# A chunked state-space scan and a two-layer MLP in one kernel: chunks 1 and 2 made one unit of work

## The chip, the core and the metric

The kernel runs on one core of a Trainium2 chip. The metric is device time in microseconds of one execution, the median over several runs. The engines are named as in the profile: PE is TensorE (PEld its weight loads), DVE is VectorE, ACT is ScalarE, POOL is GpSimd, SP is SyncE, which here only issues DMA transfers. A q after a name means the engine's instruction queue.

## What is computed

The first stage is a linear recurrence over a sequence, done in chunks; the second is a two-layer MLP with a tanh GELU on its output.

```python
batch, n_heads, seq, head_dim, d_state = (4, 8, 768, 32, 16)
n_tokens, d_model, d_ff = (3072, 256, 2048)

log_a = np.log(np.clip(a, 1e-06, 1.0))
for c in range(nc):                       # chunks of the sequence
    cum = np.cumsum(la, axis=-1)
    L = np.exp(cum[:, :, :, None] - cum[:, :, None, :]) * causal
    CB = np.einsum('bhin,bhjn->bhij', Cc, Bc)
    y_intra = np.einsum('bhij,bhjd->bhid', CB * L, xc)
    y_inter = np.einsum('bhin,bhnd->bhid', Cc, state) * np.exp(cum)[:, :, :, None]
    y[:, :, sl] = y_intra + y_inter
    Bx = np.einsum('bhjn,bhjd->bhjnd', Bc, xc) * decay_from_j[:, :, :, None, None]
    state = decay_full[:, :, None, None] * state + np.sum(Bx, axis=2)

h = x @ w_in                              # x: y with tokens as rows, 256 wide
g = 0.5 * h * (1.0 + np.tanh(c * (h + 0.044715 * h * h * h)))
out = g @ w_out
```

## The kernel before

The kernel uses its own chunk length, Q = 128, so each of the 4 batches has 6 chunks and there are 24 in all. Chunks are grouped in units: chunks 0 to 3 one by one, then pairs. `UNITS` (L120) holds the grouping, `UOF` the unit of a chunk.

The decays are not formed as exponentials of differences. For each row of a (32 batch-head rows) a reversed scan of products within a chunk gives r; C is divided by r and B multiplied by it, so that a plain product of the two with a triangular mask is already the decayed matrix. For batch 0 this is done for each half of the sequence (three chunks) separately: the four blocks of decay rows are loaded by `load_a3` (L160, DMA at L157), clipped (`f_clip3`, L304), scanned (`f_R3`, L300), transposed (`f_RT3`, L313), inverted (`f_recip3`, L317) and multiplied into C and B (`f_mul3`, L360). For batches 1 to 3 the same is done at once from `load_a12` (`f_clip12`, `f_R12`, `f_RT12`, `f_recip12`, `f_mul`).

PE then transposes C and B (`f_T3`, L371; for whole batches `f_T`, L407). The results are copied out as bh (`f_E0`, `f_E`) and, once for even and once for odd heads, as ce (`f_F0` at L389 on ACT or L391 on DVE; `f_F`). A transposed copy of bh, bn, comes from `f_N` (L426) and `f_bn`.

For each unit there follow: `f_castx` (x to 16 bits), `f_G` (the Gram product of B and C, L461, into the PSUM tile gb), `f_M` (gb times the triangular mask, L471, on DVE), `f_D` (the chunk's addition to the state, L482), `f_S` and `f_SP` (the state and its product with the block mask, L531 and L538, on DVE), `f_Y` (L504 for the part from the state, L513 for the part within the chunk, into the PSUM tile yb) and `f_yev` (its evacuation to xm, the MLP's input). `f_pe`, `f_pp` and `f_pend` form the decay of a whole chunk for the state.

gb has four banks; in each, half of the columns serve one chunk. In this version chunk 0's product goes into the left half and chunk 1's into the right half, both made in one step (`f_G(0)` calls `f_G(1)`, and `half` chooses the side).

The MLP's first layer is `f_s1` (L562): for a unit of one chunk, matmuls of 128 columns, for a pair 256; four or eight PSUM tiles per unit, each emptied by one GELU on ACT (`f_gelu`, L571). The second is `f_s2` (L580), four pieces for each chunk, then `f_oev` (evacuation) and `f_store`. The weights are loaded in 32 bits and cast to 16 by `f_wi` and `f_wo`, in eight pieces each, by POOL, ACT or DVE.

The order on each engine is not written by hand. Each step is a `Node` with an assumed duration, dependences and a priority; `run_order` simulates the engines with these durations and emits the steps in the order it finds. Dependent steps in the planner are not waits on the chip; what is emitted is each engine's order, and the chip waits by data. `TUNE` gives each step's priority by name (lower goes first among those ready), for loads (`ad_...`) too, where it overrides the order of `FIRST`; `ENG` gives the engine of a step that has a choice, and without an entry it is the first of its options: POOL for casts of weights and of x, ACT for F0 and bn and the evacuation of Y, DVE for E0 and E. All loads are issued on SP, save six of the eight row blocks of a for batch halves 0 and 1, which are issued on ACT. The loads before are in this order: C and B of the first half, w_in rows 128 to 255, x of chunk 0, w_in rows 0 to 127, x of chunk 1, C of the second half, x of chunk 2, B of the second half, the decays of all batches, two quarters of w_out, x of chunk 3, two quarters of w_out.

Where PE has nothing to do in the plan before the first `f_s1`, `idle` puts in filler matmuls (L836), one per 0.07 us of planned idle time (0.107 before 4.4 us). `paced` is a table of steps: after such a step's planned end the fillers read a tile that the step writes, and so can't start earlier on the chip. Before, the three steps are the clip, scan and transpose of the first half's decays. Fillers write a part of yb or, for a time, of gb.

Of the kernel before, what the change touches and what calls it, by code (L numbers as in the profile page):

```python
# [9 lines left out]
BF16 = mybir.dt.bfloat16  # L10
# [83 lines left out]
def kernel(  # L94
# [10 lines left out]
    nc = tc.nc  # L105
# [5 lines left out]
    NCH = batch * CPB  # L111
    HS = S // 2
    R3 = HS // 128
    R12 = S // 64
# [5 lines left out]
    UNITS = [[c] for c in range(4)] + [[c, c + 1] for c in range(4, NCH, 2)]  # L120
# [24 lines left out]
    XF, X16 = {}, {}  # L145
# [25 lines left out]

    wz = const.tile([128, 512], BF16, name="wz")
# [4 lines left out]
    for q in range(4):  # L177
        load_a3(1, q, nc.scalar)
# [274 lines left out]
    def half(u):  # L453
        return 1 if u == 1 else 0

    def f_G(u):
        if u == 0:
            f_G(1)
        for k, gc in enumerate(UNITS[u], half(u)):
            for g in range(4):  # L460
                nc.tensor.matmul(  # L461
                    out=gb[:, g, 256 * k:256 * k + 256],
                    lhsT=bh_of(gc)[32 * g:32 * g + 32],
                    rhs=ce_of(gc)[32 * g:32 * g + 32],
                    start=True, stop=True, tile_position=(32 * g, 0))

    def f_M(u, k, g0, g1):
        gc = UNITS[u][k]
        if g0 == 0:
            MT[gc] = msb.tile([128, 4, 2, Q], BF16, name="m")  # L470
        nc.vector.tensor_tensor(out=MT[gc][:, g0:g1],  # L471
                                in0=gb[:, g0:g1, 256 * (k + half(u)):256 * (k + half(u)) + 256]
                                .rearrange("p g (e t) -> p g e t", e=2),
                                in1=tri_b[:, g0:g1], op=ALU.mult)
# [145 lines left out]

    def load(dur, fn, *args, deps=()):
        nload[0] += 1
        return add("DMA", dur, fn, *args, deps=deps, done=0.9, prio=nload[0])

    win_l, won_l, wi_n, wo_n = {}, {}, {}, {}
    bl, bl3, xl, xcn = {}, {}, {}, {}
    Gn, Mn, Dn, Yn, yevn, Sn, SPn = ({} for _ in range(7))
    cen, bhn, bnn = {}, {}, {}

    a3n = load(2.6, landed, "a0")  # L630
    a3n.done = 0.8
    a3n1 = add("SP", 6.2, landed, "a1", done=0.9, prio=-1)

    FIRST = "C30 B30 i0 x0 i1 x1 C31 B31 x2 o0 x3 o1 o2 o3 A x4 x5"
    for item in FIRST.split() + [f"{t}{b}" if t in "CB" else f"x{CPB * b + int(t)}"
                                 for b in range(1, batch) for t in "CB012345"]:
        t, i = item[0], int(item[1:] or 0)
        if t in "CB" and i >= 30:
            bl3[i - 30, int(t == "C")] = load(1.0, load_bc3, i - 30, int(t == "C"))
        elif t in "CB":  # L640
            bl[i, int(t == "C")] = load(1.2, load_bc, i, int(t == "C"))
        elif t == "A":
            a12n = load(1.7, load_a12)
        elif t == "x":
            xl[i] = load(1.0, load_x, i)
        elif t == "i":
            win_l[i] = load(2.65, load_wi, i)
        else:
            won_l[i] = load(1.35, load_wo, i)
# [11 lines left out]
    for k in range(2):  # L661
        z = 60.0 * k
# [35 lines left out]
    def half_sequence(k):  # L698
        z = 40.0 * k
        t1 = add("PE", 0.2, f_T3, k, 1, deps=[mul3[k, 1], Gn.get(2)], prio=-70 + z)  # L700
        t0 = add("PE", 0.2, f_T3, k, 0, deps=[mul3[k, 0], t1], prio=-69 + z)
        if k == 0:
            T0n.append(t0)
        ev = {"ACT": 0.6, "DVE": 0.52}
        f = [add(ev, 0, f_F0, k, 0, deps=[t1], prio=-70 + z)]
        f.append(add(ev, 0, f_F0, k, 1, deps=[t1, f[0]], prio=-70 + z))
        e0 = add({"DVE": 0.52, "ACT": 0.6}, 0, f_E0, k, deps=[t0], prio=-70 + z)
        nn = add("PE", 0.2, f_N, 0, k, deps=[e0], prio=-25 + z / 4)
        bb = add({"ACT": 0.5, "DVE": 0.36}, 0, f_bn, 0, k, deps=[nn], prio=-20)
        if k:  # L710
            t1.takes("gram", *f, e0, bb)
        else:
            t1.takes("o", *f)
            t0.takes("yb", e0)
            nn.takes("hp", bb)
        for c in range(k * CPB // 2, (k + 1) * CPB // 2):
            cen[c], bhn[c], bnn[c] = f, e0, bb


    for u, cs in enumerate(UNITS):  # L720
# [8 lines left out]
        if u <= MERGE:  # L729
            gn = Gn[u] = Gn[0] if u == 1 else add(  # L730
                "PE", 0.2 + 0.11 * (2 if u == 0 else n), f_G, u, deps=cen[cs[-1]] + [bhn[cs[-1]], Gn.get(u - 1)], prio=-60 if u < 2 else q)
            Dn[u] = add("PE", 0.2 + 0.03 * n, f_D, u, deps=[bnn[cs[0]], xcn[u]], prio=q + 0.5)
            if u == 0:
                Dn[u].deps.append(Gn[u])
        else:
            gn = Gn[u] = Dn[u] = Yn[u - 1]
            gn.deps += cen[cs[-1]] + [bhn[cs[-1]], bnn[cs[0]], xcn[u]]
# [8 lines left out]
        if u == 1:  # L746
            gn.allocs[0][1].extend(ms)
        else:
            gn.takes("gram", *ms)
        Mn[u] = ms  # L750
        ss = []
        for k, gc in enumerate(cs):
            if gc % CPB == CPB - 1:
# [119 lines left out]
```

## Time and profile before

| | us |
|---|---|
| median of 13 runs | 125.15 |
| lowest and highest | 124.06, 127.96 |
| the profiled execution, its own time | 124.36 |
| span of its instructions | 122.2 |

| engine | busy us | share of the span |
|---|---|---|
| PE | 113.4 | 93% |
| PEld | 100.8 | 82% |
| ACT | 78.6 | 64% |
| DVE | 68.6 | 56% |
| POOL | 16.7 | 14% |

The profile is of one execution. The span leaves 2.16 us of that execution outside. A share of busy time is an average over the fill-in of the pipeline, the long stretch in which PE runs the MLP beside the rest, and the end. A slice of the page's second part is a fortieth of the span, 3.06 us, and its digit the busy share in tenths. PE's busy time holds the fillers too.

### The profile page before, as it was taken

What the parts mean: (1) busy time and instruction counts of PE and PEld (TensorE: products, weight loads), DVE (VectorE), ACT (ScalarE), POOL (GpSimd) and SP (SyncE); (2) the same over time, 40 slices, a digit from 0 to 9 for tenths busy, and PEclk for the clock granted to TensorE, in tenths of its full rate; (3) what the DMA queues carried; (4) which work ended last, traced back from release to release, by engine and by line L of the source; (5) the groups of instructions that cost most, each with busy time, mean ns of one, the idle gap of its engine ahead of it and who ended that gap; (6) DMA issues with size and microseconds to landing.
All of it is one profiled execution on the core that took longest, in us unless ns stands there. A gap on an engine that the chain in (4) does not pass through costs nothing.

```text
span 122.2 us, 3590 instructions
## 1 busy us (share of the span) xinstructions
PE 113.4 (93%) x1531; PEld 100.8 (82%) x1531; DVE 68.6 (56%) x127; ACT 78.6 (64%) x152; POOL 16.7 (14%) x34
## 2 busy tenths in 40 slices
PE   4992899889999999999999999999999999999990
PEld 4981787769878897998889997989898899999970
DVE  5927957999968895570899452756657200000100
ACT  4153547987674786778765675767576877678510
POOL 7204312521442042021200000000000000000000
PEclk9999769999999999999999999999999999999999
DMA  1999479999989898995011101110111011110021
GB/s 41 270 353 334 73 171 343 374 236 140 168 206 207 146 157 230 136 176 129 5 38 48 43 0 48 43 43 5 46 43 48 6 42 43 43 43 30 18 86 43
DMA packets 37199, 14.23 MB, mean 116 GB/s; under 512 B 29952, under 2 KB 36416, under 8 KB 36928
## 3 DMA queue, kind: packets, MB, share of 16 engines
q1 hardware_dynamic: 36896, 13.87, 46.3%
q8 instruction: 12, 0.20, 0.7%
q10 hardware_dynamic: 288, 0.14, 0.5%
q14 instruction: 3, 0.02, 0.1%
HBM read 10.85 MB, written 3.15 MB: 115 GB/s over the span
## 4 chain that ended last, share of the span: by engine, by line
PE 81%; DVE 7%; DMA 5%; issue 2%; ACTq 2%; ACT 1%; DVEq 0%
PE hp L562 32%; PE o_ps L580 31%; DMA a_t<-in_a_dram 5%; PE yb L580 3%; PE gb L461 3%; PE yb L513 2%; PE yb L504 2%; PE yb L836 2%; PE gb L407 2%; ACTq L157 2%; DVE r_t L300 1%; PE o_ps L562 1%; DVE sp_new L538 1%; DVE m L471 1%; PE gb L426 1%
## 5 line engine op out<-in xcount | busy, mean ns | idle before, releaser
L571 ACT ACTIVATE gT<-hp 128x512 bf16<-128x512 f32 x94 | 52.2, 596 | 18.0 <-PE hp L562 17.9
L562 PE MATMUL hp<-xm,w_in_sb 128*128 128x256 bf16 (+1 forms) x432 | 51.3, 261 | 0.0
L580 PE MATMUL o_ps<-w_out_sb,gT 128*128 128x256 bf16 x352 | 46.9, 273 | 0.5 <-DVE w_out_sb L289 0.5
L562 PEld LDWEIGHTS <-w_in_sb 128*128 128x128 bf16 x448 | 43.0, 115 | 2.9 <-issue 1.9
L580 PEld LDWEIGHTS <-gT 128*128 128x128 bf16 x384 | 37.1, 98 | 4.5 <-issue 0.7
L471 DVE TENSOR_TENSOR m<-gb,tri 128x1024 bf16<-128x1024 f32 (+1 forms) x25 | 29.3, 1172 | 1.8 <-PE gb L461 1.7
L589 DVE COPY o_sb<-o_ps 128x256 f32<-128x256 f32 x3 | 1.3, 425 | 23.4 <-PE o_ps L580 23.4
L287 POOL CAST x<-x_t 128x512 bf16<-128x512 f32 (+1 forms) x11 | 8.2, 741 | 26.0 <-DMA x_t<-in_x_dram 17.1
L285 ACT ACTIVATE xm<-yb 128x512 bf16<-128x512 f32 (+1 forms) x13 | 7.1, 548 | 5.6 <-PE hp L482 4.0
L836 PEld LDWEIGHTS <-wz 128*128 128x128 bf16 x95 | 8.5, 131 | 2.3 <-DVE warm L175 1.5
L538 DVE SCALAR_TENSOR_TENSOR sp_new<-s_new,pend,bmask 128x256 bf16<-128x256 f32 x20 | 10.2, 512 | 0.1
L531 DVE SCALAR_TENSOR_TENSOR s_new<-s_new,pend,hp 128x64 f32<-128x64 f32 x16 | 4.5, 280 | 10.0 <-PE hp L482 9.7
L836 PE MATMUL yb<-wz 128*128 128x128 bf16 x73 | 7.8, 282 | 2.0 <-DVE warm L175 1.6
L587 ACT ACTIVATE o_sb<-o_ps 128x256 f32<-128x256 f32 x19 | 7.3, 384 | 3.0 <-ACT gT L571 2.2
L513 PE MATMUL yb<-m,x 128*32 128x128 bf16 x192 | 6.3, 220 | 0.0
L504 PE MATMUL yb<-ce,sp_new 128*32 128x128 bf16 x160 | 5.4, 222 | 0.0
L399 DVE TENSOR_TENSOR bc<-bc_t,rt 128x1536 bf16<-128x1536 f32 x3 | 5.3, 1752 | 0.2 <-DMA bc_t<-in_B_dram 0.2
L461 PE MATMUL gb<-ce,bh 32*128 32x256 bf16 x96 | 5.1, 278 | 0.1
L513 PEld LDWEIGHTS <-x 128*32 128x32 bf16 x192 | 3.8, 96 | 0.7 <-issue 0.6
L504 PEld LDWEIGHTS <-sp_new 128*32 128x32 bf16 x160 | 2.8, 96 | 1.9 <-issue 1.7
L287 POOL CAST w_out_sb<-wf 128x512 bf16<-128x512 f32 x5 | 3.1, 638 | 7.6 <-DMA wf<-in_moe_w_out_dram 7.6
L289 DVE COPY ch<-gb 128x768 bf16<-128x768 bf16 x2 | 1.9, 957 | 3.7 <-PE gb L407 3.7
(78 smaller groups left out, 69.1 us busy)
## 6 DMA issues: line engine op xcount, KB each, us to landing
x_t<-in_x_dram SPq DMA_DIRECT2D x24, 128.0 KB, 4.7
out_dram<-o_sb SPq DMA_DIRECT2D x24, 128.0 KB, 1.7
wf<-in_moe_w_in_dram SPq DMA_DIRECT2D x2, 1024.0 KB, 7.7
wf<-in_moe_w_out_dram SPq DMA_DIRECT2D x4, 512.0 KB, 5.1
bc_t<-in_C_dram SPq DMA_DIRECT2D x3, 384.0 KB, 4.6
bc_t<-in_B_dram SPq DMA_DIRECT2D x3, 384.0 KB, 6.1
bc<-in_C_dram SPq DMA_DIRECT2D x2, 192.0 KB, 5.5
bc<-in_B_dram SPq DMA_DIRECT2D x2, 192.0 KB, 3.8
```

Source lines behind the costliest of these rows:

```text
L285: nc.scalar.activation(o, i, AF.Copy)
L287: nc.gpsimd.tensor_copy(out=o, in_=i)
L461: nc.tensor.matmul(out=gb[:, g, 256 * k:256 * k + 256], lhsT=bh_of(gc)[32 * g:32 * g + 32], rhs=ce_of(gc)[32 * g:32 * g + 32], start=True, ...
L471: nc.vector.tensor_tensor(out=MT[gc][:, g0:g1], in0=gb[:, g0:g1, 256 * (k + half(u)):256 * (k + half(u)) + 256] .rearrange("p g (e t) -> p ...
L504: nc.tensor.matmul(out=y4[32 * j:32 * j + 32, k, w], lhsT=sp[:, 32 * h:32 * h + 32], rhs=ce_of(gc)[:, h % 2], start=first(j), stop=False, ...
L513: nc.tensor.matmul(out=y4[32 * j:32 * j + 32, k, w], lhsT=X16[u][:, k, 32 * h:32 * h + 32], rhs=m[:, h // 2, h % 2, :], start=first(j), st ...
L538: nc.vector.scalar_tensor_tensor(out=sp_new.rearrange("p (g d) -> p g d", g=4), in0=state[("s", gc)].rearrange("p (o d) -> p o d", o=1).to ...
L562: nc.tensor.matmul(out=hp[:, j * nt:(j + 1) * nt], lhsT=w_in_sb[:, kc].rearrange("p (q m k) -> p q k m", m=128, k=4) [:, fi // 4, fi % 4], ...
L571: nc.scalar.activation(gts[u][:, i * per:(i + 1) * per, 0:nt], hps.pop((u, i)).rearrange("p (j t) -> p j t", j=per), AF.Gelu_apprx_tanh)
L580: nc.tensor.matmul(out=ops[gc], lhsT=gts[u][:, fi, tt * Q:(tt + 1) * Q], rhs=w_out_sb[:, fi, :], start=(fi == 0), stop=(fi == NF - 1), ski ...
L587: nc.scalar.activation(o_sb, ops.pop(gc), AF.Copy)
L836: nc.tensor.matmul(out=(gb[:, 3] if g_next else yb)[:, 384:384 + w], lhsT=wz[:, 0:128], rhs=r, start=True, stop=True)
```

## The change

The two chunks 1 and 2 become one unit, as the later pairs are. Chunk 0's and 1's Gram products are still made in one step; chunk 2's is made in a step of its own, into the left half after chunk 0's mask product has read it. The four row blocks of the second half's decays are issued on ACT's queue directly after those of the first half, ahead of the warm activation and its table load. Fillers are also paced by the cast of chunk 0's x, the two halves of its mask product and the eight casts of w_in. The planner is given other durations for three loads, and new tables of priorities and engines.

```diff
-    UNITS = [[c] for c in range(4)] + [[c, c + 1] for c in range(4, NCH, 2)]
+    UNITS = [[0], [1, 2], [3]] + [[c, c + 1] for c in range(4, NCH, 2)]
...
+    for q in range(4):
+        load_a3(1, q, nc.scalar)
+
     wz = const.tile([128, 512], BF16, name="wz")
...
     nc.scalar.activation(warm, warm, AF.Gelu_apprx_tanh)
-    for q in range(4):
-        load_a3(1, q, nc.scalar)
...
-    def half(u):
-        return 1 if u == 1 else 0
+    def slot(gc):
+
+        return 1 if gc == 1 else 0 if gc == 2 else UNITS[UOF[gc]].index(gc)

     def f_G(u):
-        if u == 0:
-            f_G(1)
-        for k, gc in enumerate(UNITS[u], half(u)):
+        for gc in {0: [0, 1], 1: [2]}.get(u, UNITS[u]):
+            k = slot(gc)
...
-                                in0=gb[:, g0:g1, 256 * (k + half(u)):256 * (k + half(u)) + 256]
+                                in0=gb[:, g0:g1, 256 * slot(gc):256 * slot(gc) + 256]
...
-    a3n1 = add("SP", 6.2, landed, "a1", done=0.9, prio=-1)
+    a3n1 = add("SP", 7.2, landed, "a1", done=0.9, prio=-1)
...
-            bl3[i - 30, int(t == "C")] = load(1.0, load_bc3, i - 30, int(t == "C"))
+            bl3[i - 30, int(t == "C")] = load(1.2, load_bc3, i - 30, int(t == "C"))
...
-        t1 = add("PE", 0.2, f_T3, k, 1, deps=[mul3[k, 1], Gn.get(2)], prio=-70 + z)
+        t1 = add("PE", 0.2, f_T3, k, 1, deps=[mul3[k, 1], Gn.get(1)], prio=-70 + z)
...
-    paced = {cl3n[0]: ac3[:, 0, 0:128], R3n[0]: r3_t[:, 0, 0:128],
-             RT3n[0]: rt3[:, 0].rearrange("p r b -> p (r b)")}
+    paced = {cl3n[0]: lambda: ac3[:, 0, 0:128].bitcast(BF16)[:, 1::2],
+             R3n[0]: lambda: r3_t[:, 0, 0:128].bitcast(BF16)[:, 1::2],
+             RT3n[0]: lambda: rt3[:, 0].rearrange("p r b -> p (r b)").bitcast(BF16)[:, 1::2],
+             xcn[0]: lambda: X16[0][:, 0, 0:128]}
+    for i in range(2):
+        paced[M0n[i]] = lambda i=i: MT[0][:, 2 * i, 0]
+    for q in range(4):
+        for k in range(2):
+            paced[wi_n[q][k]] = lambda q=q, k=k: w_in_sb[:, k, 512 * q:512 * q + 128]
```

By the new priorities the loads stand in this order: C and B of the first half, x of chunk 1, w_in rows 128 to 255, x of chunk 0, x of chunk 2, w_in rows 0 to 127, B and C of the second half, the decays of all batches, one quarter of w_out, x of chunk 3, three quarters of w_out.

The entries of the engine table, before and after (`wi_q_k` and `wo_q_k` are the casts of the weights in pieces; the rest of them is on POOL):

```
before  ACT: wi_0_1 wi_1_0 wi_3_1 wo_0_1 wo_3_1 castx_0 castx_1 castx_3 E_1_1 E_1_0
        DVE: wi_2_0 wo_2_0 yev_1 F0_1_1 oev_2
after   ACT: wi_1_0 wi_2_1 wi_3_0 wi_3_1 wo_3_1 E_1_1 E_1_0
        DVE: F0_0_0 F0_0_1 F0_1_0 F0_1_1 bn_0_1 bn_1_None
```

## The prediction

> **What bounds it.** I read the page's slices first, then the chain of waits, then the timeline of the first 36 us.
>
> ```profile
> PE   4992899889999999999999999999999999999990
> DVE  5927957999968895570899452756657200000100
> PEclk9999769999999999999999999999999999999999
> DMA  1999479999989898995011101110111011110021
> ```
>
> A slice is 3.06 us. From the tenth slice on TensorE (PE) never lets go; 93% of the span is PE. What can be won lies before 28 us: the fill-in of the pipeline, with a clock that drops in slices 5 and 6 (7 and 6 tenths) and a full VectorE (DVE) in slices 8 to 11. The chain, in order of time, shows how it starts:
>
> ```profile
> 3.43 6.30 DMA a_t<-in_a_dram
> 9.82 0.27 DVE ac L304
> 10.11 0.87 DVE r_t L300
> ...
> 13.93 1.64 PE yb L836 x14
> 15.57 0.33 PE gb L461 x3
> 15.90 0.98 PE o_ps L562 x8
> 16.87 1.20 PE hp L562 x16
> ```
>
> The last row block of the second half's decays is issued at 3.43 and lands at 9.73. DVE sits 1.76 us idle for it although the first Gram product ended at 8.78, so the first mask product M (L471) starts only at 11.74. Then 14 fillers (L836) run 117 ns each, and the first dense layer ("s1", L562) starts at 15.83. The windows give the clock:
>
> ```profile
> 7.10:10.50 3.40, 2.23 (x36) 1.59 (x34) 1.21 (x3) 2.04 (x5) 0.54 (x1) 1.00 1.04 373
> 10.50:13.90 3.40, 1.78 (x29) 1.48 (x30) 3.33 (x9) 1.47 (x6) 1.80 (x4) 1.00 0.84 188
> 13.90:17.30 3.40, 3.38 (x32) 2.96 (x32) 2.58 (x5) 1.19 (x3) 0.65 (x2) 0.51 0.61 121
> ```
>
> The eighth number is the clock: half speed for one stretch of 3.4 us, after one in which PE was busy 1.78 us only. Later:
>
> ```profile
> 26.95 0.43 DVE L289 CAST w_out_sb<-wf 128x512 bf16<-128x512 f32 x1
> 27.43 0.60 PE L580 MATMUL o_ps<-w_out_sb,gT 128*128 128x256 bf16 x4 [0.47 <-DVE w_out_sb L289]
> ```
>
> This w_out quarter landed at 23.9; its cast stood in DVE's queue for 3 us, and the second layer ("s2", L580) with it. Likewise the first quarter landed at 20.4, was half cast by ScalarE (ACT) at 23.42, and s2 began at 24.02.
>
> **The Trainium skill.** "TensorE: Matmul & The Clock Gate", section "What's actually happening": the clock is halved after a free-running window of about 3.4 us with too little matmul work and restored after a busy one. The windows above agree: 0.51 for 3.4 us. "DMA: Bandwidth & Descriptors", section "Queues, rings and completion order": each DMA engine takes turns between the issuing queues by packet and drains one queue in order. So rows issued on ACT do not stand wholly behind the SP loads, but share with them; the four blocks took 2.6, 3.2, 5.3 and 6.3 us, growing once w_in (1 MB, issued at 2.80) is in flight. "SBUF — State Buffer", section "Who interferes with whom": DVE operations with two SBUF inputs and GpSimd (POOL) reads exclude each other. The trace agrees: the scan takes 0.56 us alone and 0.86 beside POOL casts, the state product 0.48 and 0.82.
>
> **Part by part.**
> Decay rows: four ACT issues move ahead of the table load and the warm activation. Issues are 0.44 apart, so the sixth starts near 3.0 instead of 3.43. Landing: at best 3.0 + 5.3 = 8.3, at worst 9.7 as before; I take 8.9. The table load (1.28) slips to about 3.5 to 4.8 and the warm 0.20 to 5.0; cover is ACT's idle until 5.74.
>
> First Gram product: both copies of C (F0) go from ACT (1.05 for two) to DVE at 0.62 each (row L391), then B's copy 0.55: 7.03 + 1.79 = 8.8 against 8.06. The Gram ends 0.7 later, 9.2; hidden, since DVE clips (0.26) and scans (0.56 to 0.86) then anyway. M's two halves now stand behind the scan but before the transpose, reciprocal and pe pair: 8.9 + 0.26 + 0.86 + 1.28 + 0.15 = 11.45 done, against 13.15.
>
> Loads: x of chunk 1 goes ahead of the first w_in half, x of chunk 2 ahead of the second. Each x costs 0.43 to 0.49 where one followed w_in (10.33 after 9.9, 13.37 after 12.88). So w_in lands at 10.4 and about 13.8 instead of 9.9 and 12.88, worth +0.9 (bounds 0.5 to 1.3). B before C of the second half: both were waited for by nothing until 17.09, and their last landed at 16.8. The same loads stand before w_out; bounds for it 0.5 later to 1.5 earlier (the SP queue sat blocked while DMA moved 13 to 170 GB/s between 12.5 and 15.5). I take no change. x of chunk 3 ahead of the second w_out quarter: +0.45 there, covered as that quarter's cast ended at 23.0 and s2's second piece ran at 25.03.
>
> Casts: x of chunks 0 and 1 move from ACT to POOL, behind two w_in casts (0.61 each, 0.88 at most): 10.4 + 1.3 + 0.40 = 12.1, so Y of chunk 0 at 12.2 (was 13.08) and its evacuation at 13.0 (13.87). The last w_in casts: two on POOL, two on ACT from 13.8, first pair done 14.45; the one on DVE until 14.74 goes.
>
> Fillers: none after chunk 0's evacuation is tied to a step until w_in's last casts; I estimate some 25 of them, from about 13.1, at 56 ns (the 0.90 of 16 matmuls at 28.91), with the state-decay product pp waiting in between for DVE until about 14.4. s1 starts at 15.2; bounds 14.5 (cast alone) and 16.2 (fillers at 117 ns). Gain **0.63**. Tied to M's halves, the x cast and the w_in casts, the fillers spread over 10 to 12.3, where before there was nothing from 9.33 to 11.66. By my count of 18 fillers (1.0), products (0.5) and fillers after 13.1 (0.8), the bad window holds 2.3 us of issue instead of about 1.4. Then the clock stays up: the first 24 s1 matmuls took 0.98 + 1.20 = 91 ns each, at 56 they save 24 x 35 = **0.84**.
>
> The unit of two: Y needs both mask products, both states. DVE from 11.45: two M 2.44, transpose 0.30, reciprocal 0.29, pe pair 0.57, states 0.21 + 2 x 0.28, state products 3 x 0.48, hops 0.5 = 6.3, so Y at 17.8 and evacuation done at 19.1 (one ACT copy of 0.60 for two of 0.38 and 0.42). Chunk 1's s1 began at 19.24 before, so it loses nothing, and chunk 2's evacuation ended at 20.87: 1.7 earlier. PE waits about 1.3 us between s1 of chunk 0 (done 17.0) and 19.1. The Gram of chunk 2 goes into the half whose M is done; no cost shown or taken (0 to 0.3, waiting for a reader of the same bank). 64 narrow matmuls at 56 ns (3.58 us) become 32 of 256 columns at 109 (0.87 for 8 in the chain; 3.49): **0.09**.
>
> 19 to 28: issue work on PE from 18.07 to 28.03 was 72 x 0.056 + 12 x 0.109 + 2.1 of attention = 7.5, so 2.5 us were idle. In place of it: the 1.3 above, and 0.7 for ACT's pace (eight gelus of 0.57 for eight s1 of 0.44, s2 pieces between). w_out is cast by POOL but for one: quarters ready at 21.6, 23.1, 25.2 and 27.2, so s2 can begin 2.4 earlier and the wait on DVE at 27.43 goes. Gain 2.5 - 2.0 = **0.5**, bounds -0.4 to 1.5. ACT loses F0, x and bn work there; DVE gets the other F0 and two bn copies (0.62 + 0.49 + 0.9), loses three casts and an evacuation (0.42 each or so).
>
> Sum: 0.63 + 0.84 + 0.5 + 0.09 = 2.06. Profiled execution 124.36 (span 122.2 and 2.16 around it): 122.3. The median 125.15 lies 0.79 higher, part of it perhaps the clock window's phase that this removes; I add half: **122.7**.
>
> **Rivals.** First, a wash: PE arrives earlier and waits for chunks 4 and 5. Their x landed at 29.96 and took POOL 1.98; Y (0.45) and evacuation (0.60) make 33.0, PE would want s1 at 35.5 - 2.0 = 33.5. With x 1 us later half a us goes, with DVE's extra copies the rest; or the fillers run cold again (s1 at 16.2, no clock gain) and only the 19 to 28 gain is left. 124.2 to 125.5. For it: slack of only 0.5. Against: 1.75 us of s2 for chunk 3 lay in reserve there.
>
> Second, slower: chunk 1 is tied to chunk 2's M, last in DVE's line. If the second half's two decay products (0.55 each), the clip, the scan or its copies go ahead of it, Y slips from 17.8. It decides from about 20.3, where the old chunk 2 stood. PE has no s1 from 17.0 on; an empty stretch of over 2.3 us (the one before the drop at 13.9) costs the clock, as it did then: 3.4 us at half speed, 1.7 of work. Y at 21.5 gives 124.4 + 1.2 + 1.7 - 0.8 = 126.5. For it: DVE is full from 21.4. Against: B and C of the second half land near 16.
>
> Third, the rows don't land earlier (9.7): M done 12.3, but the x cast at 12.1 bounds Y anyway; 122.9.
>
> **Numbers.** Main case and its third variant 0.60, wash 0.13, slower 0.27. A measurement here tells about 0.5% from no change, 124.5 to 125.8. Faster 0.60, same 0.13, slower 0.27. The main case alone spans 120.6 (s1 at 14.5, idle 1.0) to 124.0; with the rivals 120.6 to 126.4.
>
> **What would show it.** Right: clip of the second half before 9.2, no clock below 0.9 after 10 us, s1 from about 15.2, no DVE casts of weights, s2 from about 21.7. Wrong: a half-speed stretch between 13 and 21, Y of the pair after 20, or PE idle near 33.

## The result, and the profile after

The change makes the kernel slower: 127.17 us median of 11 runs (125.55 to 127.92, and one at 149.82), beside 125.21 for the kernel before in 48 runs. The ratio of their runs is 1.0151, 95% interval 1.0112 to 1.0191. I had forecast 122.7 and given a slower kernel 0.27. A ratio leaves out the runs that lie well above the fastest of their own kernel, so it can part from the medians, the more so where a kernel has few runs; where the two differ below, both are given, and where they disagree on the sign no gain is taken.

The profiled execution took 127.15 us with a span of 125.3, against 124.36 and 122.2: the span is 3.1 us longer. (The execution profiled before was 0.8 faster than its median, so this pair shows some 1 us more than the medians do.) First the same four rows of the page, of the kernel after (a slice is now 3.13 us):

```profile
PE   5985888959699995999999999999999999999980
DVE  5796968981979269935499480928475300000110
PEclk9999999999999999999999999999999999999999
DMA  2998979999799799995011101100111011111021
```

In this execution the clock never falls, as I said. But TensorE is not closed from the tenth slice on as it was: slices 9, 11 and 16 are a 5, a 6 and a 5. VectorE's tenth and fourteenth slices are a 1 and a 2 (9 and 8 before), and the DMA engines are busy into the eighteenth slice, as before. What TensorE waits for between 24 and 52 us, in the kernel after (total, times, longest):

```profile
PE o_ps L581 <- POOL w_out_sb L288: 1.4, 2, 1.2
PE gb L408 <- DVE bc L400: 1.0, 1, 1.0
PE yb L514 <- DVE m L472: 0.8, 1, 0.8
PE yb L505 <- DVE sp_new L539: 0.4, 1, 0.4
```

Together 3.6 us. The same question to the trace of before gives one row, for the cast of w_out that the prediction showed:

```profile
PE o_ps L580 <- DVE w_out_sb L289: 0.5, 1, 0.5
```

So the waits of this stretch have grown by 3.1 us, as much as the span. Up to 24 us the kernel after is not behind: its second layer begins at 22.33, before at 24.02. The chain of the kernel after says what stands behind each (start, us, what):

```profile
6.17 4.52 SPq L276
...
12.49 2.59 SPq L157
...
19.81 11.04 DMA bc_t<-in_C_dram
30.97 1.77 DVE bc L400
32.78 0.84 PE gb L408 x12
...
39.12 5.91 DMA bc_t<-in_B_dram
45.06 1.76 DVE bc L400
46.82 1.13 DVE m L472
```

Where the chain of before ran over VectorE and TensorE from 10 us on, this one is a queue of loads until 31 us and again from 39 to 45. SyncE (SP) sits 4.52 us in the issue of the second half of w_in. The multiply of a batch needs its C and its B. The later of the two for batch 1 is now C, at 30.85 (before it was B, at 29.18), and for batch 2 B, at 45.03 (40.64 before). VectorE stands idle for each, with the rest of its queue behind; before, the first of these multiplies started at 29.75 without a wait. After, then before:

```profile
30.97 1.76 DVE L400 TENSOR_TENSOR bc<-bc_t,rt 128x1536 bf16<-128x1536 f32 x1 [3.27 <-DMA bc_t<-in_C_dram]
...
45.06 1.76 DVE L400 TENSOR_TENSOR bc<-bc_t,rt 128x1536 bf16<-128x1536 f32 x1 [2.24 <-DMA bc_t<-in_B_dram]
```

```profile
29.75 1.75 DVE L399 TENSOR_TENSOR bc<-bc_t,rt 128x1536 bf16<-128x1536 f32 x1
```

Why B of batch 2 is so late: the new priorities put five loads of x between C of batch 2 and it, where before there was one (its issue is at 39.12, before at 34.83). Two expectations below say seven; the trace shows five. Landing times of the early loads, read from the trace:

| landed at, us | before | forecast | after |
|---|---|---|---|
| last row block of the second half's decays | 9.73 | 8.9 | 6.25 |
| w_in, first and second half issued | 9.90, 12.93 | 10.4, 13.8 | 10.82, 15.29 |
| w_out, four quarters | 20.36, 21.62, 23.94, 25.92 | no change | 19.82, 23.85, 25.08, 27.41 |
| C and B of batch 1 | 27.56, 29.18 | not treated | 30.85, 29.39 |
| C and B of batch 2 | 38.15, 40.64 | not treated | 36.57, 45.03 |

### The profile page after: what moved, and what is told of

Its sections match the earlier page's. It is cut to its first block, busy times and chain, and to the rows that moved or that the text cites. A ratio compares the mean times of both kernels' runs of the same rounds, so it can differ in the third digit from the quotient of the medians.

```text
span 125.3 us, 3575 instructions
## 1 busy us (share of the span) xinstructions
PE 113.5 (91%) x1527; PEld 99.8 (80%) x1527; DVE 69.1 (55%) x128; ACT 75.9 (61%) x145; POOL 19.4 (16%) x38
## 4 chain that ended last, share of the span: by engine, by line
PE 62%; DMA 15%; SPq 13%; DVE 6%; issue 1%; ACT 0%; ACTq 0%; DVEq 0%
PE hp L563 25%; PE o_ps L581 25%; DMA bc_t<-in_C_dram 9%; DMA bc_t<-in_B_dram 5%; SPq L276 5%; SPq L157 3%; DVE bc L400 3%; PE yb L581 3%; PE gb L462 2%; PE yb L514 2%; DVE m L472 2%; PE yb L505 2%; PE gb L408 2%; SPq L268 2%; DMA a_t<-in_a_dram 2%; SPq L282 1%
## 5 line engine op out<-in xcount | busy, mean ns | idle before, releaser
L572 ACT ACTIVATE gT<-hp 128x512 bf16<-128x512 f32 x94 | 52.3, 596 | 17.8 <-PE hp L563 17.6
L563 PEld LDWEIGHTS <-w_in_sb 128*128 128x128 bf16 x416 | 41.4, 114 | 3.9 <-issue 1.9
L288 POOL CAST x<-x_t 128x512 bf16<-128x512 f32 (+1 forms) x13 | 9.8, 762 | 26.5 <-DMA x_t<-in_x_dram 16.6
L590 DVE COPY o_sb<-o_ps 128x256 f32<-128x256 f32 x2 | 0.8, 424 | 23.0 <-PE o_ps L581 23.0
L844 PEld LDWEIGHTS <-wz 128*128 128x128 bf16 x123 | 9.2, 115 | 3.2 <-DVE warm L178 1.5
L844 PE MATMUL yb<-wz 128*128 128x128 bf16 x74 | 6.4, 250 | 1.6 <-DVE warm L178 1.6
L288 POOL CAST w_out_sb<-wf 128x512 bf16<-128x512 f32 x7 | 4.3, 631 | 5.5 <-DMA wf<-in_moe_w_out_dram 5.5
L530 DVE COPY s_new<-hp 128x64 f32<-128x64 f32 x4 | 0.9, 225 | 7.1 <-PE hp L483 7.1
```

The costliest lines, as they stand in the source:

```text
L288: nc.gpsimd.tensor_copy(out=o, in_=i)
L563: nc.tensor.matmul(out=hp[:, j * nt:(j + 1) * nt], lhsT=w_in_sb[:, kc].rearrange("p (q m k) -> p q k m", m=128, k=4) [:, fi // 4, fi % 4], ...
L572: nc.scalar.activation(gts[u][:, i * per:(i + 1) * per, 0:nt], hps.pop((u, i)).rearrange("p (j t) -> p j t", j=per), AF.Gelu_apprx_tanh)
L844: nc.tensor.matmul(out=(gb[:, 3] if g_next else yb)[:, 384:384 + w], lhsT=wz[:, 0:128], rhs=r, start=True, stop=True)
```

## Experiments

My theory after this: the order of loads that came with the change costs the time, and the three parts that the change is named for (unit of two, early rows, pacing) do not. The main rival: the unit of two, with the copies and casts that were spread anew for it, costs it. All times below are medians beside the median of the kernel before in the same series. The series ran on five chips, and the kernel before gave 124.74 to 125.07 in them, so a difference of a few tenths between two series says nothing.

| run | edit | runs | us | before | ratio, 95% interval |
|---|---|---|---|---|---|
| e1 | after, x of chunk 2 behind w_in | 4 | 127.48 | 125.07 | 1.0161, 0.9996 to 1.0327 |
| e2 | after, B of batch 2 early | 4 | 125.50 | 125.07 | 1.0109, 1.0013 to 1.0204 |
| e3 | before, rows early | 6 | 125.50 | 125.07 | 1.0127, 1.0018 to 1.0236 |
| e4 | before, more paced steps | 20 | 124.81 | 125.07 | 1.0000, 0.9960 to 1.0040 |
| e5 | before, x of chunks 1, 2 early | 22 | 125.49 | 124.80 | 1.0042, 1.0008 to 1.0077 |
| e6 | after, all priorities of loads of before | 6 | 128.86 | 124.80 | 1.0323, 1.0254 to 1.0392 |
| e7 | after, old three paced steps | 6 | 126.39 | 124.80 | 1.0124, 1.0051 to 1.0197 |
| e8 | e3 and e4 together | 22 | 125.14 | 124.80 | 0.9928, 0.9888 to 0.9968 |
| e9 | before, B of batch 2 late | 6 | 129.81 | 125.04 | 1.0400, 1.0333 to 1.0467 |
| e10 | e5 and e9 together | 6 | 131.11 | 125.04 | 1.0482, 1.0408 to 1.0556 |
| e11 | e8, w_out ahead of later decays | 22 | 124.75 | 125.04 | 0.9928, 0.9889 to 0.9967 |
| e12 | after, both loads put back | 22 | 125.37 | 125.04 | 1.0072, 1.0038 to 1.0106 |
| e13 | before, without 1 MB of w_out | 6 | 124.49 | 125.06 | - |
| e14 | e8, without it | 6 | 121.86 | 125.06 | 0.9743, 0.9702 to 0.9784 |
| e15 | after, without it | 6 | 123.68 | 125.06 | 0.9875, 0.9835 to 0.9915 |
| e16 | e12, without it | 6 | 122.83 | 125.06 | 0.9827, 0.9784 to 0.9870 |
| e17 | e8, two w_out quarters on ACT's queue | 22 | 125.00 | 124.74 | 0.9969, 0.9913 to 1.0025 |
| e18 | e12, the same | 14 | 125.16 | 124.74 | 1.0057, 1.0019 to 1.0095 |

Where only loads move, the plan of all engines stays and SP's issues alone are permuted:

```diff
-    for t, fn in run_order(nodes, pools, idle=idle, wait=("DVE", "POOL")):
-        fn()
+    plan = run_order(nodes, pools, idle=idle, wait=("DVE", "POOL"))
+    loads = sorted((n for n in nodes if n.name.startswith("ad_")), key=lambda n: n.start)
+    want = [n.name for n in loads]
+    for m, after in MOVES:
+        want.remove(m)
+        want.insert(want.index(after) + 1, m)
...
+    plan = [swap.get(fn, fn) for _, fn in plan]
```

### One load at a time (e1, e2)

```diff
+    MOVES = [('ad_x_2', 'ad_wi_0')]             # e1, in the kernel after
+    MOVES = [('ad_bc_2_0', 'ad_bc_2_1')]        # e2, in the kernel after
```

> The changed kernel with one load moved on SP's queue: x of chunk 2 issued behind the second half of w_in instead of ahead of it; the order on every other engine stays. Theory (the load order holds the issue of w_in's second half back until the first half has landed, and everything behind it on DMA comes later): that w_in half is issued near 5.5 instead of 6.2 to 10.7, lands near 13.4 instead of 15.3, the first dense layer starts near 15.3 instead of 16.2, w_out's last quarter and C of batch 1 land 1 to 1.5 us earlier, and the time falls by 1.5 to 2.5 us. Rival (the unit of two and the copies given to DVE cost the time, not the loads): the first layer may start earlier, but the waits near 28 and 32 us stay and the time stays within 0.6 us.

> The changed kernel with one load moved on SP's queue: B of batch 2 issued directly behind C of batch 2, ahead of the x of chunk 12 and six more chunks. Theory (the two waits of PE at 48 to 50 us, 0.60 and 1.00, come from that load landing at 45.0): B of batch 2 lands before 41, both waits go, 1.6 us less. Rival (other work on DVE is the bound there): the load lands earlier and the waits remain, no change.

e2's trace did what was expected: B of batch 2 landed at 38.77, and the waits at 47 to 50, 1.2 us in the rows above, are gone. How much that is worth is less sure. The median of its four runs is 1.67 below that of the kernel after, but by the ratios (1.0109 and 1.0151, with intervals that overlap) the gain is only some 0.5. In the profiled execution the wait for the cast of w_out grew by as much as the others had been; the last quarter landed at 28.19 there, after at 27.41 (TensorE's waits, 24 to 52 us):

```profile
PE o_ps L581 <- POOL w_out_sb L288: 2.6, 2, 2.2
```

In e1 the half of w_in landed at 13.05, as expected, but the first dense layer did not follow: it began at 18.53. GpSimd takes its casts in order, and the cast of x of chunks 1 and 2 stands ahead of the last w_in casts in the plan. It now waited for the later x (landed 14.44), the w_in casts behind it ended at 16.29, and TensorE stood before the state product of that x:

```profile
PE hp L483 <- POOL x L288: 2.8, 1, 2.8
```

With the clock gone too, e1's start is 2.4 us later than that of the kernel after; yet its profiled execution took 125.55, less than the 127.15 of after. It is the fastest of e1's four, whose median (127.48) is no better than that of the kernel after, so no gain is shown. But within this one execution the start comes later and the end sooner: a first sign that the start does not set the end.

### The other two parts alone (e3, e4, e7, e8)

```diff
     for q in range(4):
         load_a3(0, q, nc.scalar if q in (1, 2) else nc.sync)
+    for q in range(4):                          # e3 and e8, in the kernel before
+        load_a3(1, q, nc.scalar)
...
-             xcn[0]: lambda: X16[0][:, 0, 0:128]}        # e7, in the kernel after
-    for i in range(2):
-        paced[M0n[i]] = lambda i=i: MT[0][:, 2 * i, 0]
-    for q in range(4):
-        for k in range(2):
-            paced[wi_n[q][k]] = lambda q=q, k=k: w_in_sb[:, k, 512 * q:512 * q + 128]
```

(e4 and e8 put these paced steps into the kernel before.)

> The kernel before with the four row blocks of the second half's decays issued ahead of the warm activation, nothing else. Theory: the rows land near 6.3 instead of 9.7, the first mask product starts near 9 instead of 11.7, but SP's loads start some 0.5 us later (as in the changed kernel, where B of the first half was issued at 2.71 instead of 2.17) and w_in's landing still sets the first layer: between -0.6 and +0.5 us. Rival (the rows were the bound, as the chain has it): the first layer starts a us earlier and the time falls by 1 us.

> The kernel before with the fillers paced by the eight w_in casts, the x cast and the two halves of the first mask product, nothing else. Theory: the fillers spread over 9.7 to 14, the clock does not fall, the first 24 matmuls of the first layer take 56 ns instead of 91: -0.8 us. Rival: fillers tied to late casts hold PE back as much as they win: no change.

> The kernel after with fillers tied to the three old steps only (clip, scan and transpose of the first half), not to the mask products, the x cast and the w_in casts. Theory (the fillers keep the clock): a stretch of about 3.4 us at half speed returns between 10 and 20 and the time rises by 0.5 to 1.5 us over the kernel after. Rival (the early rows alone, which bring PE real work sooner, or the loads set the start whatever the clock): clock at full speed or lost where PE waits anyway, time within 0.4 us of the kernel after.

> The kernel before with the early decay rows and the extended pacing both, but chunks 1 and 2 as two units and the old plan: the change without its unit of two, its new order of loads and its new spread of the copies. Theory (the order of the loads that came with the unit costs the time): s1 starts at 14 to 14.5 with the clock up, time 0 to 1.5 us below before (123.6 to 125.1). Rival (the rows on ACT's queue cost what they bring, by later loads on SP): second half of w_in and the w_out quarters land 0.5 to 1 later, time 0.3 to 1.5 us above before.

None of these moves the time by more than its scatter. (e8 is 0.7% faster by its ratio and 0.3 us slower by its median; e7 is 0.8 below the median of the kernel after.) In e3's profiled execution, the fastest of its six (123.31), the rows landed at 8.31, not near 6.3, but brought what they should: the first mask product at 9.73, the first dense layer at 14.08 with the clock up, 1.75 us before the 15.83 of the kernel before. At the end 1.0 of it is left (a span of 121.2 against 122.2), although the profiled execution of the kernel before had also lost the clock. The rest is given back (TensorE's waits in e3, 20 to 36 us, and the multiply of batch 1 on VectorE):

```profile
PE o_ps L581 <- POOL w_out_sb L288: 1.2, 1, 1.2
PE gb L408 <- DVE bc L400: 0.4, 1, 0.4
```

```profile
28.90 1.76 DVE L400 TENSOR_TENSOR bc<-bc_t,rt 128x1536 bf16<-128x1536 f32 x1 [2.06 <-DMA bc_t<-in_B_dram]
```

e8's profiled execution did not start early: its first dense layer came at 15.66, with the clock fallen, and not at 14 to 14.5.

Pacing: e4's clock fell all the same, e8's in its profiled execution too, and e7, without the new pacing, kept it in half of its executions. The mean clock of each timed execution is at least 0.995 in 11 of the 156 of the kernel before, in 3 of 20 of e4, in 4 of 12 of after and in 3 of 6 of e7. So the clock is kept more often with the change, perhaps by the earlier work (e3, with the rows alone, keeps it in 2 of 6); that the extra paced steps do it is not shown, and e7 speaks against it. Over the 156 executions of before, the 11 with the clock up have a median of 124.0, those below 0.975 one of 125.14: by this comparison, which is no experiment, it is worth about 1.1 us.

### The mirror, in the kernel before (e5, e9, e10), and a whole replanning (e6)

```diff
+    MOVES = [('ad_x_1', 'ad_bc3_0_0'), ('ad_x_2', 'ad_x_0')]   # e5
+    MOVES = [('ad_bc_2_0', 'ad_x_14')]                         # e9; e10 has all three
```

(e5 and e10 also emit the first nine loads ahead of everything else, which changes no engine's order but SP's.)

> The kernel before, with nothing changed but the order in which SP issues the first loads: x of chunk 1 ahead of the first half of w_in and x of chunk 2 ahead of the second half, as in the kernel after. Theory (the queue of loads): the second half's issue is held on SP until the first half drains, near 10; it lands at about 15 instead of 12.93, s1 starts at about 17.5 instead of 15.83, the first w_out quarter lands no earlier; time about +1.5 us (126 to 127). Rival (the loads have slack, and the loss of the kernel after comes from the unit of two and DVE's extra copies): the second half lands by 13.8, s1 starts by 16.5, time within 0.5 us of before.

> The kernel before with B of batch 2 issued behind the x of chunk 14 instead of ahead of it, as late in the queue as in the kernel after; nothing else. Theory (B of batch 2 costs where its multiply is due at 41 to 43): it lands at 43 to 45 instead of 40.64, VectorE waits 2 to 4 us for it, TensorE waits 1 to 2 us for Y near 47, time +0.8 to +1.8. Rival (the wait in the kernel after came from its own later chunks, a late load alone is absorbed): no wait of TensorE over 0.3 us near 47, time within 0.4 of before.

> The kernel before with both changes of the loads' order: x of chunks 1 and 2 ahead of the w_in halves, and B of batch 2 behind x of chunk 14. Units, rows, pacing and the spread of the copies stay. Theory (the loads' order is the loss): the sum of the two single ones, 0.7 and 0.8 to 1.8, so +1.5 to +2.5: the time of the kernel after (126.3 to 127.3). Rival (they overlap, a later start hides a later B, or the unit of two costs on its own): +0.3 to +1.0.

> The kernel after with the loads' priorities of the kernel before, so that the planner puts x of chunks 1 and 2 behind the w_in halves again and B of batch 2 right behind its C; unit of two, early rows and pacing stay. Theory (the loads' order is the loss): the second half of w_in is issued before 6 and lands at 12.9 to 13.5, s1 starts by 15.2, no wait near 48, time 1.5 to 3 us below the kernel after (124 to 125.5). Rival (the unit of two and DVE's copies): s1 starts early but Y of the pair comes after 18.5 and the same waits follow at 26 to 32; time within 0.7 of the kernel after.

e5 reproduces the held issue in the kernel before. SP's queue in e5 (start, us, engine, line; the issue of the second half of w_in is the last row):

```profile
3.43 1.22 SPq L275 DMA_DIRECT2D wf<-in_moe_w_in_dram  x1
4.77 1.36 SPq L267 DMA_DIRECT2D x_t<-in_x_dram  x2
6.17 3.51 SPq L275 DMA_DIRECT2D wf<-in_moe_w_in_dram  x1
```

Before, that issue took 0.35 us and ended at 5.03. In e5 it ends at 9.69, 0.22 before the first half lands (9.91), and the second half lands at 15.27 instead of 12.93. But the price is 0.7 us (0.5 by the ratio, 1.0042), not the 1.5 expected. The first dense layer came at 16.24, only 0.4 after that of the kernel before: there, the last cast of w_in ended at 14.74, but TensorE ran fillers at half speed until 15.8. So most of this delay was hidden. e5 shows one thing more: the last block of the second half's decays landed at 6.33 instead of 9.73, though it was issued at the same 3.4. What is new is that w_in was issued no sooner than that block, at 3.43 instead of 2.80.

e9 overshoots the other way: +4.8, where I expected at most 1.8. B of batch 2 landed at 44.70, VectorE waited 3.61 for it at the head of its queue, and behind its multiply stood the state update (L531) that frees the PSUM tile hp for the first dense layer. TensorE's wait, and then three windows of 3.4 us with the clock as the eighth number:

```profile
PE hp L562 <- DVE s_new L531: 2.7, 1, 2.7
```

```profile
40.80:44.20 3.40, 3.40 (x65) 2.75 (x62) 0.31 (x1) 2.35 (x6) 0.62 (x1) 1.00 0.84 174
44.20:47.60 3.40, 0.70 (x8) 0.49 (x6) 2.84 (x4) 0.44 (x1) 2.17 (x2) 1.00 0.93 203
47.60:51.00 3.40, 3.40 (x22) 2.62 (x20) 2.44 (x4) 2.50 (x5) 0.00 (x0) 0.61 1.23 216
```

One empty window, and the next runs at 0.61. The transposes of batch 2 (L407) start at 56.83, 5.0 later than before's 51.80. So the same late load costs 0.5 to 1.7 us in the kernel after and 4.8 in the kernel before: its price depends on what VectorE has queued behind it and on whether TensorE's wait is long enough to lose the clock. So that load alone can cost more than the whole loss. e10 adds 1.3 to e9, and ends well above the kernel after: the two orders of loads do more harm in the plan of before than in the plan that they came with.

e6 misses with both theories. Its half of w_in was early (13.57), its first dense layer at 15.28, but the planner drew the whole of batch 2 forward: TensorE's transposes for it start at 44.30 (54.41 in after), and VectorE waits 2.61 for a B that lands at 41.26. The priorities are one plan together; half of them taken from another plan is a third plan. It tells nothing of the cause.

### The kernel after mended (e12), and w_out moved up (e11)

```diff
+    MOVES = [('ad_x_2', 'ad_wi_0'), ('ad_bc_2_0', 'ad_bc_2_1')]     # e12
+    mv('castx_1', 'wi_2_0')      # the cast of x of chunks 1, 2 behind the last w_in cast on POOL
+    mv('D_1', 's1_0_1')          # and what needs it behind the first dense layer of chunk 0
...                                # (three more moves: the states behind D_1)
+    MOVES = [('ad_a12', 'ad_wo_1')]                                 # e11, in e8
```

> The kernel after with both loads put back in the issue order alone (x of chunk 2 behind the second half of w_in, B of batch 2 behind C of batch 2), and, so that nobody stands behind the later x, its cast on GpSimd behind the w_in casts and its state product and states behind the first s1 of chunk 0. Unit of two, early rows, pacing and copies stay. Theory (the loads' order is the loss): second half of w_in lands at about 13.1, s1 starts by 14.8, no wait near 48; time 124 to 125.3, no slower than before. Rival (the unit of two costs on its own): Y of the pair after 18.5, TensorE idle over 1.5 us between chunk 0's s1 and the pair's, time 126 or more.

> The kernel before with early rows and extended pacing (the run e8), and the first two quarters of w_out issued ahead of the decay rows of batches 1 to 3 (four small loads) instead of behind them. Theory (an earlier start is given back at w_out): the first quarters land 1 to 1.5 earlier (18.0 and 19.5), s2 begins near 21 to 23, the clip of the later batches is not late; time 0.3 to 1.5 below e8. Rival (the last quarter and C and B of batch 1 gate, and they are moved by the sum of the bytes, not by their order): last quarter still at 25 to 26, C and B of batch 1 at 28 and 29.5; time within 0.3 of e8.

e12 is faster than the kernel after, by 1.8 us by the medians and 1.0 by the ratios, whose intervals do not overlap, and no faster than before (1.0072, 1.0038 to 1.0106). Its start is 2.7 us before that of the kernel after: the first dense layer at 13.49, with the clock up in the whole profile. It is given back (TensorE's waits, 24 to 52 us):

```profile
PE o_ps L581 <- POOL w_out_sb L288: 2.0, 1, 2.0
PE gb L408 <- DVE bc L400: 0.9, 1, 0.9
PE hp L483 <- POOL x L288: 0.8, 1, 0.8
```

The last quarter of w_out landed at 27.11 and C of batch 1 at 30.44; the third wait is new, an x that now lands at 41.66. e11 started at 13.51, but its w_out quarters landed at 19.36 and 20.68, no earlier than e8's 19.49 and 20.80 though issued 3 us sooner, and the decays behind them were 4 us late (VectorE waited 2.6 for them). Its median is 0.3 below before; by its ratio it is 0.7% faster, as e8 is too, so the new order of w_out brings nothing that shows.

### The loads taken away (e13 to e16), and moved to another queue (e17, e18)

```diff
     def load_wo(q):
+        if q >= 2:                              # e13 to e16
+            WF["o", 1] = WF["o", 0]
+            return
...
-        nc.sync.dma_start(out=WF["o", q // 2]
+        (nc.scalar if q < 2 else nc.sync).dma_start(out=WF["o", q // 2]     # e17, e18
```

> The kernel before without the loads of the last two quarters of w_out (1 MB); their casts read the first two quarters instead, so every other instruction stays. It is the base for the next three. Theory (loads up to 30 us are a bound, with little slack in before): C and B of batch 1 land some 3 to 4 us earlier (24 to 26), and the time falls a little, by 0.3 to 1.3. Rival (the engines' plan is the bound): within 0.3 of before.

> The run e8 (before with early rows and extended pacing) without the loads of the last two quarters of w_out. Theory (the early start is given back at the loads): now the start is kept; 0.8 to 2.0 us below e13. Rival (the plan of the engines gives it back): within 0.4 of e13, as e8 was within 0.4 of before.

> The kernel after without the loads of the last two quarters of w_out. Theory: no wait at 25 to 32, but w_in still lands late; B of batch 2 behind seven x is some 3 us less late, so the wait near 48 shrinks; 0.5 above to 1.0 below e13, so at least 1.5 of the 2 us between after and before goes. Rival (the unit of two and the spread of the copies cost): still 1.5 to 2.5 above e13.

> The run e12 (the kernel after with x of chunk 2 and B of batch 2 put back) without the loads of the last two quarters of w_out. Theory (its early start, 13.5, was lost only at w_out and at C and B of batch 1): 1.0 to 2.5 below e13, the fastest of the four. Rival (the unit of two and the spread of the copies cost): 0.3 to 0.9 above e13, as e12 stood to before.

> The run e8 (before with early rows and extended pacing), with the first two quarters of w_out issued by ScalarE behind its second-half w_in cast, near 14, instead of by SP behind the decay rows. Theory (one queue held by its own earlier loads leaves the DMA engines half idle from 12 to 15 us): the first quarter lands at 17.5 to 18.5 instead of 19.5, C and B of batch 1 0.5 to 1.5 earlier than 28.1 and 29.4; time 0.4 to 1.5 below e8 and below before. Rival (the bytes are the limit, whichever queue has them): the rows of the later batches and B of the second half land later by as much, C and B of batch 1 within 0.4; time within 0.3 of e8.

> The run e12 (the kernel after with x of chunk 2 and B of batch 2 put back), with the first two quarters of w_out issued by ScalarE behind its third w_in cast, near 13, instead of by SP. Theory (as for e17): the second quarter lands at 20 to 21 instead of 22.5, the last one at 25.5 to 26.5 instead of 27.1, the wait at 25 shrinks from 2.25 to under 1.2; time 0.5 to 1.3 below e12, so at or below before. Rival (the bytes are the limit): last quarter and C of batch 1 within 0.4; time within 0.3 of e12.

e13 to e16 leave out the last two quarters of w_out and cast the first two a second time, so only their times mean anything. Without this 1 MB of the loads, the kernel before gains 0.6, the kernel after 3.5, e8 3.3 and e12 2.5 (each against its own median with all loads). The clearest pairs are the kernel after with e15, and e12 with e16, since the clock is up in all four profiled executions. The first dense layer starts at 16.15 in the kernel after and at 15.98 in e15, yet e15's span is 4.1 us shorter (121.3). e16 starts it 1.3 later than e12 (14.76) and is still 3.0 shorter (121.0 against 124.0). So neither the start nor the clock, but the transfers, cost these. The 2.0 us that the kernel after loses to before with all loads are gone without these: e15's median is 0.8 below that of e13, which is less than their runs scatter.

For e14 the clock has a larger part. Its median is 2.6 below e13, its span 1.7. Its clock mean is at least 0.995 in all 6 executions, as in e16 and in 5 of 6 of e15, but in none of e13 and in 5 of 22 of e8; why the shorter queue keeps it up I can't say. By the 1.1 us above, the clock explains up to two thirds of this. The first dense layer starts 0.63 sooner (14.65 against 15.28), and that start is no longer given back. VectorE's multiply for batch 1, in e13, in e14 and in e15:

```profile
29.75 1.75 DVE L401 TENSOR_TENSOR bc<-bc_t,rt 128x1536 bf16<-128x1536 f32 x1
```

```profile
27.72 1.75 DVE L402 TENSOR_TENSOR bc<-bc_t,rt 128x1536 bf16<-128x1536 f32 x1
```

```profile
27.57 1.75 DVE L402 TENSOR_TENSOR bc<-bc_t,rt 128x1536 bf16<-128x1536 f32 x1
```

In e13 C and B of batch 1 land at 23.2 and 25.1 and the multiply still starts at 29.75, just as in the kernel before: there the engines set it. In e14 it starts 2 us sooner, 0.5 after B lands (27.20); e15 no longer waits for it, where the kernel after stood 3.27 us. With all loads and the order of before for them, the later of the two is there at 28.5 to 31.5 and never sooner (before, e3, e4, e8, e9, e11, e17), although the first dense layer starts anywhere from 13.35 to 15.83 in these runs; e3 waits 2.06 us for it and e17 1.06. So the kernel before sits near a balance: its engines reach that multiply at 29.75 and its loads are done at 29.18. What comes earlier on the engines is then paid back, in large part, in waiting.

There is a remainder. I had expected e16 to be the fastest of the four, but it is 1.0 above e14 (0.6 by the spans), with the clock up in all executions of both. e16 has the unit of two and e14 has not, and between 14 and 24 us its trace has a wait of TensorE that e14's has not:

```profile
PE yb L507 <- DVE sp_new L541: 0.9, 1, 0.9
```

It stands in Y of the pair, before the part of chunk 2, for VectorE's product of chunk 1's state; in e14 chunk 1 goes into its first dense layer by itself at that time. e12 has the same wait of 0.9. So the unit of two seems to cost about that when nothing hides it. e16 also has other copies and another order of loads than e14, and no run has the unit alone.

e17 and e18 gained nothing. In e17 the quarters issued by ScalarE landed at 19.02 and 22.62 (19.49 and 20.80 in e8), C and B of batch 1 at 27.42 and 28.64 (28.05 and 29.39, a difference within their spread); in e18 the last quarter landed at 27.20 (27.11 in e12). The Trainium skill, "DMA: Bandwidth & Descriptors", section "Issuing engines are not separate DMA queues", says that transfers run on the same engines whoever issues them and that only the sequencer's time is saved; these runs agree. So what binds before 30 us is, as far as the runs show, the amount of the transfers and not which queue holds w_out. With all its loads, no version here is faster than the kernel before by more than the medians and the ratios can agree on (0.3 us, e11).

## Why the prediction was wrong

**What came as forecast.** The rows landed early (6.25, below my bound of 8.3: w_in was issued 1 us later and no longer shared with them; by e5 this alone brings 6.33, by e3 the earlier issue alone 8.31). The clip of the second half was at 8.22, M ran from 8.98, and the mask products of chunks 0 and 1 were done at 11.37, where I had chunk 0's alone done at 11.45. The clock stayed up in the profiled execution. Y of chunk 0 came at 12.79 (I said 12.2), Y of the pair at 17.16 (17.8), s2 at 22.33 (21.7). No weight cast is left on VectorE. The slower rival that I named, a late Y of the pair, did not happen; slower came by another way. Of the signs of being wrong one came: TensorE stood idle before 32.8, for C of batch 1.

**The step that failed first: w_in, "+0.9 (bounds 0.5 to 1.3)".** I counted the bytes of one x ahead of each half, 0.43 to 0.49 us apiece. It was +2.4 (15.29 against 12.93), because the two x in front also moved the second issue behind the point where SP can still get rid of it. The issue lasted 4.52 us, until 0.14 before the first half landed, and meanwhile nothing else was queued. e5 holds it likewise with this order alone, and in e1, with one x moved back, the half landed at 13.05. Slice 4 of the kernel after moved 154 GB/s, ahead of the second half's landing; before, the like gap came in slice 5 (73 GB/s), when that half was in. The gain of 0.63 at s1 went to -0.3 (16.15 against 15.83). I had seen SP "sat blocked" in the trace of before and drew no conclusion from it.

**What I left out of the sum: B of batch 2.** That it stands behind five more x than its C was in the diff's priorities and not in my working; by e2 it costs 0.5 to 1.7 us, and e9 shows that it can cost more. I counted moved transfers for the loads in front only.

**The step under all the others: "what can be won lies before 28 us".** I took the three gains there (0.63, 0.84, 0.5) to be gains at the end. The transfers that must land by 30 us end at about the same time whatever the engines do (not before 28.5 in any run with all loads), and before's own slack was 0.57 us (B of batch 1 at 29.18, its multiply at 29.75). I had nearly this in the wash rival ("slack of only 0.5", for x of chunks 4 and 5) and gave it 0.13. That I took no change for w_out failed too: its second, third and last quarter came 2.2, 1.1 and 1.5 us later.

**Sizes.** The clock's 0.84 was about right where it is kept (1.1 by the runs), but before keeps it in 7% of executions and after in a third, so my estimate of its worth in the median is some 0.3. The unit of two I had at a gain of 0.6 (0.5 and 0.09); the one comparison that can see it, e16 against e14, puts it at a loss of 0.6 to 1.0, with a wait of 0.9 in Y of the pair. The prediction has that wait as "about 1.3 us", inside a net gain of 0.5.

**The account.** It does not close to tenths. Of the 2.0 us, the two loads together are 1.0 to 1.8 (e12, with the casts that had to move along). B of batch 2 alone is 0.5 to 1.7 of that (e2, four runs); x of chunks 1 and 2 early is 0.5 to 0.7 by e5 in the kernel before, and what it is in the kernel after is not shown. The rest, 0.3 to 0.9, stays in e12; the unit's wait of 0.9 is a candidate for it, not shown to be it.

## What to carry to other kernels

Before an earlier start is counted as a gain, ask which transfer the work must next wait for, and by how much that one is early: that slack, not the time saved, caps the gain. When priorities are drawn anew, list every load by its issue and landing and check each against the instruction that takes it, far down the queue as well. To find out whether transfers or engines give a gain back, take some bytes away from both kernels and look whether the difference appears.

## What the runs showed of the hardware

- An issue on SP can last until about when a large load still in flight lands: in the kernel after 4.52 us (ended 10.68, landing 10.82), in e5 3.51 us (9.69, 9.91), in the kernel before 3.62 us for a small load of C (9.70, 9.90). In all 20 traces one issue on SP, the ninth or tenth, ends 0.01 to 0.22 us before the first half of w_in lands, whatever it loads. Whatever is behind it in the queue waits as well. Not every issue is held so: in the kernel before the second half of w_in, as the seventh, took 0.35 us with the first half in flight. What fills up is not shown.
- With six issues in a row on ScalarE, B of the first half was issued at 2.71 instead of 2.17. This was no slower issue but a wait of SP's queue for the first block of decay rows on ScalarE's queue, which landed at 2.69; in the trace both transfers signal through one semaphore, and in the kernel before B has one that nothing used before it:

```profile
SPq L259 <- DMA a_t<-in_a_dram: 0.6, 1, 0.6
```

- The same order of loads lands with a spread of 1 to 2 us between executions: the last quarter of w_out at 25.92 in before, 27.23 in e9 and 27.97 in e4, with the same loads ahead of it.
- A stretch of 3.4 us with TensorE busy for 0.70 was followed by one at 0.61 of the clock (e9); stretches with 2.26 and 2.46 busy cost nothing (after). The edges of the stretches were chosen in the trace.
